# Weight folding moved to a third PSUM bank and one slot later, one ring for all weight buffers, and a later turn of the second half's rows

## The chip, the cores and the metric

The kernel runs on one core of a Trainium2 chip. The metric is the time of one execution on the device, in microseconds (us).

## The reference, cut to what matters

Three layers follow each other. The first is a gated linear attention (4 batches, 8 heads, 768 steps, head size 48): a state per head decays by a gate and takes up one outer product in each step.

```python
state = f[t] * state + k[t] (outer) v[t];  y[t] = q[t] @ state      # f = sigmoid(f_logit)
x = y as 3072 rows of 384
h = x @ w_in                      # 384 x 2048
x2 = (h * sigmoid(h)) @ w_out     # 2048 x 384
e = argmax(x2 @ w_gate)           # one of 8 experts for each row
out = prob(e) * (max(x2 @ w1[e], 0) @ w2[e])   # 384 x 1024 x 384
```

The matrices `w_in` and `w_out` of the second layer come as 64-bit floats, the others as 32-bit floats.

## The kernel before, in words

Every product of the second and the third layer is made of three products of parts: each operand is split in a rounded high part (ACT copies it) and a low part (the difference, on DVE, for some weights on POOL). So a weight buffer is always a pair, hi and lo.

**Second layer.** The 24 chunks of 128 rows form 9 groups (2, 2, six times 3, 2 chunks). A slot is one step of the second layer: nine matmuls of the first product for one slice of 128 hidden columns (`moe_h`, into one of two banks "h"), then the second product of the slice of two slots before (`moe_o`, into the banks `px` of kind "x", one for each chunk). There are 144 slots. The order is group 0 with slices 0 to 7, group 1 with slices 0 to 15, group 0 with slices 8 to 15, then the other groups. PSUM's eight banks are two "h", three "x" and three "a"; the groups 0 and 1 hold two of the three "x". What else has to be done is entered in a plan by slot: `at(slot, ...)` puts it behind the nine matmuls of `moe_h`, `at_end(slot, ...)` behind `moe_o`. The matmuls of PE run in the order in which the program writes them (`ORD = 1`). The instructions of the other engines are put in order by a scheduler which simulates times, except those that are wrapped in `keep`.

**Attention.** Six stages for each chunk run in slots ahead of the chunk's group; they use the banks "a" (the first two chunks also "h").

**Weights of the second layer.** `load_piece` fetches one slice of 128 columns of `w_in` or 128 rows of `w_out`, narrows the 64-bit numbers on DVE in three instructions, and splits. Four slices make a unit, with one buffer for hi and one for lo. The first of the three narrowing instructions is kept in program order for slices below `PI` and `PO` (12); the others are placed by the scheduler. In the profile the kept one carries L201 and the free one L320.

**Folding.** So that the second product gives the gate's logits with it, each of the 16 slices of `w_out` gets eight more columns, the slice times `w_gate`: `fold_turn` transposes the slice with six matmuls into a bank, ACT copies it (L264) into `wturn`, `fold_gate` multiplies it by `w_gate` with six matmul instructions into the same bank, then ACT writes the high part (L273) and DVE the low part (L274) of the result into the weight buffer. Slice i is folded in slot i + 3 (i below 8) or i + 11. The groups from 2 on use these columns; the logits of the groups 0 and 1 are made otherwise.

**Third layer.** The rows are scattered (POOL, `route`) into slots by expert. The largest expert known early (item 0) is begun before the second layer is at an end: its first 256 slots are the "head", its other 256 the "rest". The head's eight `up` steps and two `down` steps are written between the last steps of the second layer by the string `TAIL`: o is `moe_o`, f the next step of the head, F all that are left of them, p and r the routing of the last group, w the loading of the next expert's first weights, k the ranking of the other experts, g the fetch of the rest's rows from the slots (`xe_r`), t the turn of these rows: six transposes on PE into banks (`pxs_r`), copied by ACT and DVE to `x_r`. Then `moe2` does the rest's `up` (`p_r`) and `down` and the other experts.

**Buffers.** Weight pairs come from two rings of eight buffers each, "wa" for `in` and `w1`, "wb" for `out` and `w2` (and one buffer for `x_r`). A new unit takes the buffers that come next in its ring, once their last reader is done. The rows of the second layer's result (`x2`) rotate through five buffers.

Of the kernel before, what the change touches and what calls it, by code (L numbers as in the profile page):

```python
# [9 lines left out]
F32 = mybir.dt.float32  # L10
F32R = mybir.dt.float32r
# [10 lines left out]
P = 128  # L22
CAP = 512
ROW = 388
# [5 lines left out]
FA = 1  # L30
FB = 3
# [1 line left out]
ORD = 1  # L33
AMP = ()
STP = (1, 2, 3, 4, 5, 6, 7)
PI = 12
PO = 12
LF = -27
LV = -16
KACT = 7  # L40
ND = 1
MO = 'oeh'
TAIL = 'ofofpffrffwgffktfF'
KW = -14
HF0 = 137
FX = 0
# [45 lines left out]
def kernel(  # L92
# [16 lines left out]
    NT, DM = out.shape  # L109
    DFF = moe_w_in.shape[1]  # L110
    E, _, F2 = moe2_w1.shape
    KC = DM // P
# [12 lines left out]
    HF = NF // 2  # L125
# [5 lines left out]
    dram = ctx.enter_context(tc.tile_pool(name="dram", bufs=1, space=DRAM))  # L131
    main = ExitStack()
    ps = main.enter_context(tc.tile_pool(name="ps", bufs=1, space=PSUM))
    wts = main.enter_context(tc.tile_pool(name="wts", bufs=8))
    raw = main.enter_context(tc.tile_pool(name="raw", bufs=4))
    phase = ExitStack()
    att = phase.enter_context(tc.tile_pool(name="att", bufs=1))
    late = phase.enter_context(tc.tile_pool(name="late", bufs=1))

    def bank(kind, name):  # L140
        return ps.tile([P, 512], F32, tag=kind, name=name, bufs={"h": 2, "x": 3, "a": 3}[kind])
# [19 lines left out]
    wgc = const.tile([P, KC, E], F32, name="wgc")  # L161
# [5 lines left out]
    wturn = [side[:, ROW + i * DM : ROW + (i + 1) * DM] for i in range(2)]  # L167
# [30 lines left out]
    units = {}  # L198

    def keep(fn):  # L200
        return lambda *a, **k: tc.keep_in_program_order(fn(*a, **k))  # L201

    def new_unit(key):
        kind = key[0]
        full = [P, 4, KC, P] if kind in ("in", "w1") else [P, 4, DM + E if kind == "out" else DM]
        nm = "_".join(str(x) for x in key)
        tag = "wa" if kind in ("in", "w1") else "wb"
        units[key] = tuple(wts.tile(full, F32R, tag=tag, name=f"{nm}_{x}") for x in ("hi", "lo"))

    def part_of(src, kind, i, n):  # L210
        cols = slice(i * P, (i + n) * P)
# [15 lines left out]
    def load_piece(kind, i):  # L227
        u, h = divmod(i, 4)
        src = moe_w_in if kind == "in" else moe_w_out
        nm = f"{kind}_{i}"  # L230
        if h == 0:
            new_unit((kind, u))
        shape = [P, KC, P] if kind == "in" else [P, 1, DM]
        if src.dtype == I64:
            t = raw.tile(shape + [2], U32, tag="raw", name=f"{nm}_raw")
            made = len(pieces_made)
            pieces_made.append(i)
            load_raw(t.rearrange("p c f w -> p c (f w)"), src, kind, i, nc.scalar if made < RAW else nc.sync)
            x = raw.tile([P, ROW], U32, tag="cv", name=f"{nm}_cv", bufs=2)[:, :DM].rearrange("p (c f) -> p c f", c=shape[1])
            t2 = t.rearrange("p c f w -> p (c f) w")  # L240
            pin = keep if i < (PI if kind == "in" else PO) else lambda fn: fn
            narrow(t2, x.rearrange("p c f -> p (c f)"), pin)
            x = x.bitcast(F32)
        else:
            x = raw.tile(shape, F32, tag="raw", name=f"{nm}_raw")
            nc.sync.dma_start(out=x, in_=part_of(src, kind, i, 1))
        split((kind, u), h, x if kind == "in" else x[:, 0], nc.vector)
# [6 lines left out]
    folding = {}  # L254

    def fold_turn(i):
        u, h = divmod(i, 4)
        pt = bank("a", f"pe_{i}")
        for c in range(KC):
            for j, part in enumerate(units["out", u]):  # L260
                pe.matmul(
                    pt[:, c * P : (c + 1) * P], part[:, h, c * P : (c + 1) * P], identr, start=j == 0, stop=j == 1
                )
        nc.scalar.copy(wturn[i % 2], pt[:, :DM])  # L264
        folding[i] = pt

    def fold_gate(i):
        u, h = divmod(i, 4)
        hi, lo = (a[:, h, DM : DM + E] for a in units["out", u])
        o = folding.pop(i)[:, DM : DM + E]  # L270
        for c in range(KC):
            pe.matmul(o, wturn[i % 2][:, c * P : (c + 1) * P], wgc[:, c, :], start=c == 0, stop=c == KC - 1)
        nc.scalar.copy(hi, o)  # L273
        nc.vector.tensor_sub(lo, o, hi.bitcast(F32))  # L274

# [42 lines left out]
    def narrow(r, x, pin=lambda fn: fn):  # L318
        top, low = r[:, :, 1], r[:, :, 0]
        pin(nc.vector.tensor_scalar)(  # L320
            out=x, in0=top, scalar1=3, scalar2=0x3FFFFFF8, op0=ALU.logical_shift_left, op1=ALU.bitwise_and
        )
        nc.vector.scalar_tensor_tensor(
            out=x, in0=top, scalar=0xC0000000, in1=x, op0=ALU.bitwise_and, op1=ALU.bitwise_or
        )
        nc.vector.scalar_tensor_tensor(
            out=x, in0=low, scalar=29, in1=x, op0=ALU.logical_shift_right, op1=ALU.bitwise_or
        )
# [204 lines left out]
    def moe_o(g, i):  # L533
        hi, lo = gt.pop((g, i))
        first, last = ((0, HF), (HF - 1, NF - 1)) if g == 0 else ((0,), (NF - 1,))
        wh, wl = units["out", i // 4]
        if i in first:
            px[g] = [bank("x", f"px_{g}_{t}") for t in range(sizes[g])]
        for t in range(sizes[g]):
            w = DM if g < 2 else DM + E  # L540
            o = px[g][t][:, :w]
            m = slice(t * P, (t + 1) * P)
            pe.matmul(o, hi[:, m], wl[:, i % 4, :w], start=i in first, stop=False)
            pe.matmul(o, lo[:, m], wh[:, i % 4, :w], start=False, stop=False)
            pe.matmul(o, hi[:, m], wh[:, i % 4, :w], start=False, stop=i in last)
        if i in last:
            moe_x2(g, i)

    x2 = {}
    lgt = {}  # L550

    def moe_x2(g, i):
        lgt[g] = att.tile([P, sizes[g], E], F32, tag="lg", name=f"lg_{g}", bufs=2)
        for t in range(sizes[g]):
            n = starts[g] + t
            if n in x2:
                nc.vector.scalar_tensor_tensor(
                    out=x2[n][:, :DM], in0=px[g][t][:, :DM], scalar=0.5, in1=x2[n][:, :DM], op0=ALU.mult, op1=ALU.add
                )
                r = x2[n]  # L560
            else:
                r = att.tile([P, ROW], F32, tag="x2", name=f"x2_{n}", bufs=5)
                x2[n] = r
                if g < NG - 1 and t != 1:
                    nc.scalar.activation(r[:, :DM], px[g][t][:, :DM], AF.Copy, scale=0.5)
                else:
                    nc.vector.tensor_scalar(out=r[:, :DM], in0=px[g][t][:, :DM], scalar1=0.5, scalar2=None, op0=ALU.mult)
            if g >= 2:
                nc.vector.tensor_scalar(
                    out=lgt[g][:, t, :], in0=px[g][t][:, DM : DM + E], scalar1=0.5, scalar2=None, op0=ALU.mult  # L570
                )
            if dbg is not None and "x2" in dbg and i == NF - 1:
                nc.sync.dma_start(out=dbg["x2"][n * P : (n + 1) * P, :], in_=r[:, :DM])
        del px[g]
# [230 lines left out]
    def slots_of(k, t, n):  # L805
        return xs.rearrange("(n p) d -> n p d", p=P)[bass.ds(expert[k] * (CAP // P) + t, n)]
# [18 lines left out]
    def rest_fetch():  # L825
        nt = CAP // P - HEAD
        w = nt * P
        r = [raw.tile([P, ROW], F32, tag="cv", name=f"xe_r_{t}", bufs=2) for t in range(nt)]
        for t in range(nt):
            keep(nc.sync.dma_start)(out=r[t], in_=slots_of(0, HEAD + t, 1).rearrange("n p d -> p (n d)"))  # L830
        x = wts.tile([P, 2, KC, w], F32R, tag="wb", name="x_r")
        items["rest"] = dict(nm="r", e=0, w=w, rows=lambda t: r[t], x=[x[:, i] for i in range(2)])

    def moe2(m2):
# [267 lines left out]
    def at(slot, fn, *args):  # L1102
        plan.setdefault(slot, []).append((fn, args))

    def at_end(slot, fn, *args):
        after.setdefault(slot, []).append((fn, args))

    for n in range(NCH):
        g, r = group_of[n]
# [22 lines left out]
    for j in range(2 * NF):  # L1132
        s = VS + j * VD // 2
# [12 lines left out]
            at(s0 + RD + 3, lambda: load_ids(ranks[0], (0, 1)))  # L1146
    assert s0 + RD < len(seq)
    for i in range(NF):
        at(i + (3 if i < HF else 11), fold_turn, i)
        at_end(i + (3 if i < HF else 11), fold_gate, i)  # L1150
    def head_turn():
        head_start()
        turn(items["head"])
# [57 lines left out]
    def fill(n):  # L1211
        for fn, i in ops[:n]:
            fn(items["head"], i)
        del ops[:n]

    def preload():
# [4 lines left out]
        o=lambda: moe_o(*outs.pop(0)), f=lambda: fill(1), F=lambda: fill(len(ops)),  # L1221
        p=lambda: pick(g), r=lambda: route(g), w=preload, k=rank_rest,
        g=rest_fetch, t=lambda: turn(items["rest"]),
    )
    for c in TAIL:
        todo[c]()
# [47 lines left out]
```

## Time and profile before

| | |
|---|---|
| runs (3) | 872.99 us median, 872.1 to 876.35 |
| profiled execution | 878.09 us |
| its span | 876.4 us |
| mean granted clock of TensorE | 0.962 |
| PE busy | 839.1 us (96%) |
| DVE, ACT, POOL busy | 492.3, 383.6, 109.9 us |

The profiled execution took 1.7 us more than its span, and 5.1 us (0.6%) more than the median of the runs. A granted clock of 1.0 is 2.4 GHz, one of 0.5 is 1.2 GHz.

### The profile page before, as it was taken

What the parts mean: (1) busy time and instruction counts of PE and PEld (TensorE: products, weight loads), DVE (VectorE), ACT (ScalarE), POOL (GpSimd) and SP (SyncE); (2) the same over time, 40 slices, a digit from 0 to 9 for tenths busy, and PEclk for the clock granted to TensorE, in tenths of its full rate; (3) what the DMA queues carried; (4) which work ended last, traced back from release to release, by engine and by line L of the source; (5) the groups of instructions that cost most, each with busy time, mean ns of one, the idle gap of its engine ahead of it and who ended that gap; (6) DMA issues with size and microseconds to landing.
All of it is one profiled execution on the core that took longest, in us unless ns stands there. A gap on an engine that the chain in (4) does not pass through costs nothing. (4 is left out here: it accounts for less than half of the span.)

```text
span 876.4 us, 15480 instructions
## 1 busy us (share of the span) xinstructions
PE 839.1 (96%) x5696; PEld 801.3 (91%) x5696; DVE 492.3 (56%) x1307; ACT 383.6 (44%) x815; POOL 109.9 (13%) x144
## 2 busy tenths in 40 slices
PE   6889989999999999999999999999799999999994
PEld 3789989998999999999999999998798999999994
DVE  6886578365666565665565665366456146246520
ACT  5554455345345345345445333355245245345520
POOL 2000000000111001002001001048100110111011
PEclk9667979999999999999999999999899999999997
DMA  9763336412235325326324332314173425425400
GB/s 198 170 157 108 74 111 222 142 37 53 73 85 127 95 69 131 85 59 132 80 62 118 91 72 82 100 37 155 36 235 122 138 91 192 140 96 190 162 24 27
DMA packets 166437, 95.95 MB, mean 109 GB/s; under 512 B 115692, under 2 KB 159965, under 8 KB 166352
## 3 DMA queue, kind: packets, MB, share of 16 engines
q1 hardware_dynamic: 162224, 83.80, 36.3%
q0 software_dynamic: 3280, 9.49, 3.0%
q10 hardware_dynamic: 848, 1.57, 0.6%
q8 instruction: 47, 0.77, 0.4%
q14 instruction: 38, 0.31, 0.1%
HBM read 75.61 MB, written 16.33 MB: 105 GB/s over the span
## 5 line engine op out<-in xcount | busy, mean ns | idle before, releaser
L355 PE MATMUL px<-out_lo,gh 128*128 128x392 f32 (+1 forms) x384 | 137.8, 359 | 0.0
L519 ACT ACTIVATE se<-ph 128x384 f32<-128x384 f32 (+1 forms) x144 | 65.3, 454 | 160.6 <-PE ph L355 151.1
L355 PE MATMUL px<-out_hi,gl 128*128 128x392 f32 (+1 forms) x384 | 132.1, 344 | 1.6 <-DVE gl L530 1.6
L355 PE MATMUL px<-out_hi,gh 128*128 128x392 f32 (+1 forms) x384 | 131.7, 343 | 0.0
L521 DVE SCALAR_TENSOR_TENSOR sg<-se,ph 128x384 f32<-128x384 f32 (+1 forms) x144 | 72.8, 506 | 98.2 <-ACT se L519 98.1
L355 PE MATMUL ph<-xtl,in_hi 128*128 128x384 f32 (+1 forms) x384 | 125.0, 325 | 0.0
L355 PE MATMUL ph<-xth,in_hi 128*128 128x384 f32 (+1 forms) x384 | 124.0, 323 | 0.0
L355 PE MATMUL ph<-xth,in_lo 128*128 128x384 f32 (+1 forms) x384 | 123.8, 323 | 0.0
L530 DVE TENSOR_TENSOR gl<-sg,gh 128x384 fp32r<-128x384 f32 (+1 forms) x144 | 79.8, 555 | 36.9 <-ACT gh L529 35.8
L529 ACT CAST gh<-sg 128x384 fp32r<-128x384 f32 (+1 forms) x144 | 68.6, 477 | 64.7 <-DVE sg L521 60.7
L355 PEld LDWEIGHTS px<-out_lo,gh 128*128 128x128 f32 x384 | 73.1, 190 | 2.4 <-ACT gh L529 0.2
L355 PEld LDWEIGHTS px<-out_hi,gl 128*128 128x128 f32 x384 | 73.1, 190 | 2.3 <-DVE gl L530 2.3
L355 PEld LDWEIGHTS px<-out_hi,gh 128*128 128x128 f32 x384 | 72.9, 190 | 0.0
L355 PEld LDWEIGHTS ph<-xtl,in_hi 128*128 128x128 f32 x384 | 72.6, 189 | 0.2
L355 PEld LDWEIGHTS ph<-xth,in_hi 128*128 128x128 f32 x384 | 72.6, 189 | 0.0
L355 PEld LDWEIGHTS ph<-xth,in_lo 128*128 128x128 f32 x384 | 72.6, 189 | 0.0
L355 PE MATMUL po<-w_lo,hh 128*128 128x384 f32 (+6 forms) x200 | 68.0, 340 | 0.0
L251 ACT CAST w_hi<-w_raw 128x384 fp32r<-128x384 f32 x124 | 57.2, 514 | 23.5 <-DMA w_raw<-in_moe_w_dram 22.5
L355 PE MATMUL po<-w_hi,hh 128*128 128x384 f32 (+6 forms) x200 | 67.3, 336 | 0.0
L355 PE MATMUL po<-w_hi,hl 128*128 128x384 f32 (+6 forms) x200 | 67.3, 336 | 0.0
L252 DVE TENSOR_TENSOR w_lo<-w_raw,w_hi 128x384 fp32r<-128x384 f32 x104 | 52.8, 550 | 11.7 <-ACT w_hi L251 11.5
L355 PE MATMUL p<-xsl,w_hi 128*128 128x480 f32 (+6 forms) x168 | 58.6, 349 | 0.0
(256 smaller groups left out, 1586.6 us busy)
## 6 DMA issues: line engine op xcount, KB each, us to landing
w_raw<-in_moe_w_dram SPq DMA_DIRECT2D x64, 384.0 KB, 4.4
xs<-side SPq DMA_DIRECT2D x8, 776.0 KB, 4.6
out_again<-in_moe_w_out_dram SPq DMA_DIRECT2D x16, 384.0 KB
xe<-xs SPq DMA_DIRECT2D x7, 776.0 KB, 6.1
out_raw<-in_moe_w_out_dram SPq DMA_DIRECT2D x13, 384.0 KB
f<-in_f_logit_dram SPq DMA_DIRECT2D x24, 192.0 KB, 3.7
k<-in_k_dram SPq DMA_DIRECT2D x24, 192.0 KB, 3.4
q<-in_q_dram SPq DMA_DIRECT2D x24, 192.0 KB, 3.0
```

The lines of the kernel that those rows point to most:

```text
L251: (keep(nc.scalar.copy) if key == ("w1", 1, 1) and RT > 1 else nc.scalar.copy)(hi, x)
L252: lo_engine.tensor_sub(lo, x, hi.bitcast(F32))
L355: ins = nc.tensor.matmul(*a, **k)
L519: nc.scalar.activation(e, ph[:, :GT], AF.Tanh, scale=0.5)
L521: nc.vector.scalar_tensor_tensor(out=t, in0=e, scalar=1.0, in1=ph[:, :GT], op0=ALU.add, op1=ALU.mult)
L529: (nc.scalar.copy if g < GACT else nc.vector.tensor_copy)(hi, t)
L530: (nc.gpsimd if (g, i) < LOV else nc.vector).tensor_sub(lo, t, hi.bitcast(F32))
```

## The change

Folding takes its bank from kind "x" instead of "a", and each slice is folded one slot later (`FA` = 4, `FB` = 12). Its last two instructions, of ACT and DVE, are now a function of their own, `fold_put`, which is still called right behind `fold_gate`. The first narrowing instruction is kept in program order for all 16 slices of both matrices. The two rings of weight buffers become one of 16, so that a unit takes the buffers of the oldest unit of either kind. The rows `x2` rotate through four buffers. In `TAIL` the turn of the rest's rows (t) moves behind one more step of the head (f), which is the first of its two `down` steps.

```diff
-PI = 12
-PO = 12
+PI = 16
+PO = 16
+FA = 4
+FB = 12
...
-TAIL = 'ofofpffrffwgffktfF'
+TAIL = 'ofofpffrffwgffkftF'
...
-    wts = main.enter_context(tc.tile_pool(name="wts", bufs=8))
+    wts = main.enter_context(tc.tile_pool(name="wts", bufs=16))
...
-        tag = "wa" if kind in ("in", "w1") else "wb"
-        units[key] = tuple(wts.tile(full, F32R, tag=tag, name=f"{nm}_{x}") for x in ("hi", "lo"))
+        units[key] = tuple(wts.tile(full, F32R, tag="wt", name=f"{nm}_{x}") for x in ("hi", "lo"))
...
-        pt = bank("a", f"pe_{i}")
+        pt = bank("x", f"pe_{i}")
...
     def fold_gate(i):
         u, h = divmod(i, 4)
+        o = folding[i][:, DM : DM + E]
+        for c in range(KC):
+            pe.matmul(o, wturn[i % 2][:, c * P : (c + 1) * P], wgc[:, c, :], start=c == 0, stop=c == KC - 1)
+
+    def fold_put(i):
+        u, h = divmod(i, 4)
         hi, lo = (a[:, h, DM : DM + E] for a in units["out", u])
         o = folding.pop(i)[:, DM : DM + E]
-        for c in range(KC):
-            pe.matmul(o, wturn[i % 2][:, c * P : (c + 1) * P], wgc[:, c, :], start=c == 0, stop=c == KC - 1)
         nc.scalar.copy(hi, o)
         nc.vector.tensor_sub(lo, o, hi.bitcast(F32))
...
-                r = att.tile([P, ROW], F32, tag="x2", name=f"x2_{n}", bufs=5)
+                r = att.tile([P, ROW], F32, tag="x2", name=f"x2_{n}", bufs=4)
...
-        x = wts.tile([P, 2, KC, w], F32R, tag="wb", name="x_r")
+        x = wts.tile([P, 2, KC, w], F32R, tag="wt", name="x_r")
...
-        at(i + (3 if i < HF else 11), fold_turn, i)
-        at_end(i + (3 if i < HF else 11), fold_gate, i)
+        s = i + (FA if i < HF else FB)
+        at(s, fold_turn, i)
+        at_end(s, fold_gate, i)
+        at_end(s, fold_put, i)
```

## Rows read from the trace of the kernel before

**Rows 1.** The page: busy time by engine; granted clock in 40 slices (tenths).

```profile
PE 839.1 (96%) x5696; PEld 801.3 (91%) x5696; DVE 492.3 (56%) x1307; ACT 383.6 (44%) x815; POOL 109.9 (13%) x144
...
PEclk9667979999999999999999999999899999999997
```

**Rows 2.** Waits of PE, whole span: us in total, times, longest us.

```profile
PE py L355 <- DVE am L422: 5.9, 7, 2.5
PE pxs_r L360 <- DMA xe_r<-xs: 4.9, 1, 4.9
...
PE px L355 <- DVE gl L530: 1.6, 2, 1.2
...
PE pe L355 <- DVE xtl L500: 0.5, 1, 0.5
```

**Rows 3.** Windows: length, busy us of PE, PEld, DVE, ACT, POOL; clock; DMA.

```profile
58.30:75.15 16.85, 16.85 (x80) 16.00 (x79) 10.79 (x26) 6.56 (x18) 0.00 (x0) 0.50 0.47 120
...
117.80:129.70 11.90, 9.39 (x42) 9.14 (x41) 9.35 (x22) 3.03 (x9) 0.24 (x1) 0.58 0.34 86
...
625.70:631.60 5.90, 5.86 (x20) 5.57 (x21) 1.27 (x3) 1.12 (x3) 0.00 (x0) 0.50 0.00 1
```

**Rows 4.** Timeline of PE, end of second product, first expert: start us, length us.

```profile
620.55 0.28 PE L355 MATMUL p_h<-xeh_h,w_hi 128*128 128x256 f32 x1
625.68 1.84 PE L360 MATMUL pxs_r<-identr,xe_r 128*128 128x128 f32 x6 [4.86 <-DMA xe_r<-xs]
627.18 0.67 PE L355 MATMUL po_h<-w_lo,hh_big 128*128 128x384 f32 x1
...
633.47 0.34 PE L355 MATMUL po_h<-w_lo,hh_big 128*128 128x384 f32 x1
...
638.05 0.39 PE L355 MATMUL p_r<-x_r,w_hi 128*128 128x256 f32 x1
```

**Rows 5.** Timeline of POOL: the last group's scatters into the slots.

```profile
619.33 0.99 POOL L674 DMA_INDIRECT xs<-x,r_idx  x1 [5.50 <-DVE r_idx L667]
620.62 0.97 POOL L674 DMA_INDIRECT xs<-x,r_idx  x1 [0.30 <-issue]
```

**Rows 6.** Timeline of DVE: head's last hidden part; low parts of the rest's rows.

```profile
621.28 0.42 DVE L764 SCALAR_TENSOR_TENSOR in_q_h<-p_h,hh_side 128x256 fp32r<-128x256 f32 x1
...
627.11 1.28 DVE L750 TENSOR_TENSOR x_r<-pxs_r,x_r 128x256 fp32r<-128x256 f32 x3 [4.81 <-ACT x_r L749]
```

**Rows 7.** Windows, folding's instructions alone: one turn and gate at either clock.

```profile
64.25:65.42 1.17, 1.17 (x6) 1.17 (x6) 0.00 (x0) 0.00 (x0) 0.50 1.02 255
67.45:68.58 1.13, 1.13 (x6) 1.13 (x6) 0.00 (x0) 0.00 (x0) 0.50 0.00 0
97.53:98.25 0.72, 0.72 (x6) 0.72 (x6) 0.00 (x0) 0.00 (x0) 1.00 0.00 0
99.34:99.92 0.58, 0.58 (x6) 0.58 (x6) 0.00 (x0) 0.00 (x0) 1.00 0.65 131
```

**Rows 8.** Timeline of PE: one folding gate and the next fold's turn.

```profile
137.28 0.79 PE L355 MATMUL pe<-wgc,side 128*128 128x8 f32 x6
...
139.03 0.22 PE L355 MATMUL pe<-identr,out_hi 128*128 128x128 f32 x1
```

**Rows 9.** Timeline of DVE: narrowing of late pieces, and a fold's low part.

```profile
133.17 0.35 DVE L320 TENSOR_SCALAR out_cv<-out_raw 128x384 uint32<-128x384 uint32 x1
...
134.57 0.35 DVE L320 TENSOR_SCALAR in_cv<-in_raw 128x384 uint32<-128x384 uint32 x1
...
138.66 0.15 DVE L274 TENSOR_TENSOR out_lo<-pe,out_hi 128x8 fp32r<-128x8 f32 x1
```

**Rows 10.** Timeline of ACT: first conversion of the first expert's weights.

```profile
579.21 0.93 ACT L251 CAST w_hi<-w_raw 128x384 fp32r<-128x384 f32 x2 [0.68 <-PE ph L355]
```

**Rows 11.** Timeline of PE: end of the first output unit's last use; expert's start.

```profile
584.47 0.28 PE L355 MATMUL ph<-xtl,in_hi 128*128 128x256 f32 x1
...
610.17 0.38 PE L355 MATMUL p_h<-xel_h,w_hi 128*128 128x256 f32 x1 [0.52 <-DVE xel_h L750]
```

## The prediction

> **What bounds the kernel now.** I read the page first, then the waits of PE, then tables of windows over the stretches where PE waits or its clock is low, and at last the timelines of those stretches. The page says that PE is busy for 96% of the span, and no other engine for more than 56% [rows 1]. So the time is PE's own work, plus the time in which PE has nothing to do, plus what the granted clock costs. The row of the clock shows where that cost lies: in the first seven slices of 21.9 us and around slice 29 [rows 1]. Of the waits [rows 2] the longest single one, 4.9 us, is the turn of the rest's rows for their fetch. The waits for `am` and for `gl` belong to steps that the change leaves where they are; the 0.5 us of a folding turn for an attention bank belong to the change. Two clock stretches touch it too: 58.3 to 75.15 us at half clock, with folding in it, and 625.7 to 631.6 us, right behind the long wait [rows 3].
>
> **The turn of the rest's rows.** The last matmul of the head's last `up` starts at 620.55, and the turn's row counts 4.86 us of idle ahead of 625.68, so the idle begins at 620.82. Then PE stands still until 625.68, when the rows are there, turns them until 627.18, runs the first `down` until 633.47 and the second, with the small matmul of the flags behind it, until the rest's first `up` at 638.05 [rows 4]. That is 17.2 us. The six transposes took 1.50 us and the first `down` 6.29, since most of it ran at 0.5 [rows 3, 4]; the second `down` ran at full clock, and it and the flags took 638.05 - 633.47 = 4.58 us. The other `down`, 24 matmuls of the same shapes, then costs about 4.2 us at full clock, and the transposes about 0.75 (half of 1.50).
>
> With the change the first `down` starts at 620.8. Its last input is made at 621.28 + 0.42 = 621.70 [rows 6] and is needed only in its last three matmuls, so it isn't held up. It ends at 625.0. The rows land when they did: the two scatters start on POOL at 619.33 and 620.62, released by the index that DVE made [rows 5], and the fetch on SP's queue follows the second; none of them waits for PE's later steps. PE waits from 625.0 to 625.68, 0.7 us. In this trace waits of 1.2 us (for `gl`) and less passed inside stretches at full clock [rows 1, 2], so I take the clock to stay up. Turn to 626.4, second `down` and flags to 631.0: the rest's first `up` starts 638.05 - 631.0 = 7.1 us earlier. The copies of ACT and DVE behind the turn now have the 4.2 us of one `down` to hide in instead of two; in the trace the last low part was made at 627.11 + 1.28 = 628.39 [rows 6], 2.7 us behind the start of the turn. Everything behind (the write of the head's rows, the next fetches) hangs on the end of the second `down` and moves with it. Bounds: 7.8 us if the rows come 0.7 earlier; 4.1 us if the clock falls all the same (the half of a 5.9 us stretch given back).
>
> **Folding.** No instruction goes or comes. A turn costs 1.17 us at half clock and 0.72 at full, the six gate matmuls 1.13 and 0.58 [rows 7]. Slot 3 loses a fold and slot 11 gets one; slot 3 lies around the start of the low stretch, slot 11 at full clock. So about one fold changes from low to full clock: 2.30 - 1.30 = 1.0 us gained. The second eight folds move within full clock: nothing. The wait for an attention bank, 0.5 us [rows 2], goes. What comes is a wait that the trace of before doesn't show. With two "x" banks held by `px`, every fold uses the same third bank, so a turn must wait for the ACT and DVE instructions of the fold before. Where DVE is fullest the low part ended at 138.66 + 0.15 = 138.81 and the next turn began at 139.03 [rows 8, 9]: 0.2 us of room. Two such DVE instructions more in front (0.35 each) would make a wait of 0.5 us. I take 0.5 us in all, between nothing and 16 times 0.5 = 8 us, since the turn also has the nine matmuls of its own slot in front, as before. Sum of folding: 1.0 + 0.5 - 0.5 = 1.0 us gained. The `px` banks of the next group open only behind the nine matmuls of a slot, and their two copies fit in there: nothing. A bank of kind "a" that is free earlier may let attention start earlier; I take nothing.
>
> **Pieces in program order.** In the trace the free narrowing instructions stand nearly in that order already: only one piece of `w_out` runs before the last of `w_in`, by 1.4 us [rows 9]. Nothing, with 1.4 us either way as bounds. Behind a pinned instruction DVE's queue of `sg` and `gl` would stand, and PE behind them.
>
> **One ring.** The first expert's first unit takes the buffers of the oldest `out` unit, not of the oldest `in` unit. It was converted from 579.21 on [rows 10]; the last reader of that `out` unit ends at 584.47 [rows 11], so this starts 5.3 us later. PE needs the unit at 610.17 [rows 11], and POOL, which makes the low parts, is free for 5.50 us ahead of the scatters [rows 5]. So it's hidden; without that cover the scatters and then the turn come later, at worst by 5 us, of which the moved `down` doesn't hide any more. The units behind it take buffers freed earlier or as early, but for the first `w2` unit, two slots later, which POOL converts later still. Rows `x2` in four buffers: three are taken at a group's end, when those of the group before have been scattered for some nine slots. Nothing.
>
> **Sum.** 7.1 + 1.0 = 8.1 us: 878.1 to 870.0 for the profiled execution. It lay 5.1 us above the median of the runs, and the terms don't depend on that, so I take them from the median: 873.0 - 8.1 = 864.9.
>
> **Rivals.** (a) Faster still: the clock comes back earlier in the stretch from 58.3 to 75.15. In it the gate's tiny matmuls stand between dense blocks; with the first fold out of slot 3 the dense block there gets longer. If the clock rises 10 us earlier, half of that is gained: 860. For it: at 625.7 dense work ended the low clock after 5.9 us [rows 3], in the fold stretch it took 16.85. Against: DVE is full there, and PE may wait instead.
> (b) The tail's gain comes, and the early part gives it back: the scheduler orders ACT and DVE anew, and a wait like the one at 117.8 appears. That window of 11.9 us had a mean clock of 0.58 and PE busy 9.39 us [rows 3]; at full clock its work takes about 5 us: the price is 7. Result 872, no change.
> (c) The rows of the rest land later, because the conversions on POOL slide 5.3 us and reach into the scatters: they take 4 us of the gain, result 869. Against it are the 5.50 us [rows 5].
> (d) Slower: the single bank decides. If DVE is behind in most folds, 16 waits of 0.5 us are 8 us, and PE's small idles in that part let the clock fall once or twice, at 5 us each (11.9 times 0.42, [rows 3]): 873 - 8.1 + 8 + 10 = 883. It decides from about 0.8 us for each of 16 folds on, which is 12.8 us, the sum plus 0.5%. For it: the room is 0.2 us at one place [rows 8, 9]; against: elsewhere DVE is idle for much of the stretch, 10.79 of 16.85 us busy [rows 3].
>
> The Trainium skill (TensorE: Matmul & The Clock Gate, section "A second HAM failure mode: psum-queue depth-cycling") speaks against this change. It tells of a kernel that cycled through PSUM banks, where short idles between groups of matmuls were enough to swing the clock. By that rule (d) is what happens, at 883 instead of 864.9. No row of before shows such a swing: folding ran there with the clock at 1.0 [rows 7] as well as at 0.5.
>
> **How the numbers follow.** Forecast 0.45, (a) 0.2, (b) 0.17, (c) 0.08, (d) 0.1. The predicted time is the forecast's, 865. The range reaches from (a), less 2 us for the spread of the runs, to (b): 858 to 872. It leaves out (d) and the tails of (a). Forecast, (a) and half of (c) and a little of (b) are faster by more than 0.5% (under 868.6; less can't be told from no change): 0.71. Slower is (d), less some of it: 0.08. The rest, 0.21, is no change.
>
> **What would show it.** Right: the first `down` of the head follows its last `up` without idle, the turn's wait is below 1 us, and the clock stays at 1.0 until the rest's first `up`, 10 to 11 us behind the head's last `up`. Folding's turns wait for L274 for under 1 us in all. Conversions of the first expert's weights start near 584 and PE's expert start doesn't wait for them. Wrong: a turn wait of 3 us or more, a low clock behind it, waits of folding turns for L274, or a new low stretch ahead of 170 us.

## The result, and the profile after

| | before | after |
|---|---|---|
| runs | 872.99 us median | 865.6 us median (864.64 to 866.23) |
| ratio, with its 95% interval | | 0.9908 [0.9882, 0.9933] |
| profiled execution | 878.09 us | 865.60 us |
| its span | 876.4 us | 863.9 us |
| mean granted clock | 0.962 | 0.975 |
| PE busy | 839.1 us | 826.0 us |

The changed kernel is 0.9% faster, 7.4 us between the medians. One of its five executions took 2391.78 us; the range and the ratio leave it out, nothing on record says what slowed it, and none of the seven executions run later was like it. The two profiled executions lie 12.5 us apart. In the page of the changed kernel (busy time by engine, clock in 40 slices) more of the early slices are high than in [rows 1], and the dip at slice 29 is gone:

```profile
PE 826.0 (96%) x5696; PEld 790.2 (91%) x5696; DVE 492.2 (57%) x1307; ACT 384.0 (44%) x815; POOL 109.9 (13%) x144
...
PEclk8789979999999999999999999999999999999997
```

The third and fourth slice are at 8 and 9 where [rows 1] has 6 and 7, and the slice with the tail is at 9 instead of 8. The waits of PE (in total, times, longest) show what became of the turn's wait:

```profile
PE py L360 <- DVE am L427: 6.8, 9, 1.8
PE pl L360 <- ACT lfh L353: 3.3, 1, 3.3
PE px L360 <- DVE gl L535: 3.1, 3, 2.5
...
PE pxs_r L365 <- DMA xe_r<-xs: 0.9, 1, 0.9
PE pk L365 <- ACT qt L407: 0.7, 1, 0.7
```

The turn waited 4.9 us in [rows 2] and waits 0.9 here. This list of all waits down to 0.7 us has no line with `pe`: no folding turn waited for the fold before it, nor for an attention bank.

The timeline of PE over the tail answers to [rows 4]:

```profile
615.33 0.28 PE L360 MATMUL p_h<-xeh_h,w_hi 128*128 128x256 f32 x1
615.44 0.34 PE L360 MATMUL po_h<-w_lo,hh_big 128*128 128x384 f32 x1
...
620.73 1.15 PE L365 MATMUL pxs_r<-identr,xe_r 128*128 128x128 f32 x6 [0.95 <-DMA xe_r<-xs]
621.64 0.42 PE L360 MATMUL po_h<-w_lo,hh_big 128*128 128x384 f32 x1
...
626.31 0.39 PE L360 MATMUL p_r<-x_r,w_hi 128*128 128x256 f32 x1
```

The first `down` starts right behind the head's last `up`, and the turn follows it. A window over the same stretch (length, busy time of PE and the others, clock) has PE busy for 9.97 of 11 us, all of it at full clock, where [rows 3] has 5.9 us at 0.5:

```profile
615.40:626.40 11.00, 9.97 (x59) 9.02 (x58) 2.52 (x13) 2.13 (x6) 1.96 (x2) 1.00 0.28 92
```

Three differences make up the 12.5 us. The head's last `up` starts at 615.33 against 620.55 [rows 4], so 5.2 us were already there ahead of the tail. From that matmul to the rest's first `up` it is 10.98 us against 638.05 - 620.55 = 17.50: 6.5 us. From there to the span's end it is 237.6 us against 238.35: 0.8 us. The 7.4 us between the medians leave no room for the first term as a gain of the change. That was the first thing to settle.

### The profile page after: what moved, and what is told of

Same layout as the page of the kernel before. It is cut to its first block, busy times and chain, and to the rows that moved or that the text cites. A ratio compares the mean times of both kernels' runs of the same rounds, so it can differ in the third digit from the quotient of the medians.

```text
span 863.9 us, 15479 instructions
## 1 busy us (share of the span) xinstructions
PE 826.0 (96%) x5696; PEld 790.2 (91%) x5696; DVE 492.2 (57%) x1307; ACT 384.0 (44%) x815; POOL 109.9 (13%) x144
## 4 chain that ended last, share of the span: by engine, by line
PE 66%; issue 10%; DMA 10%; DVE 5%; ACT 4%; SPq 2%; POOL 1%; POOLq 0%; DVEq 0%; ACTq 0%
PE px L360 20%; PE ph L360 19%; DMA out_dram<-o,oi 6%; PE p L360 5%; PE py L360 5%; PE po L360 4%; PE pe L360 2%; PE sc L360 2%; POOL w_lo L253 1%; PE pl L360 1%; PE pq L365 1%; PE p_r L360 1%; PE pk L365 1%; PE po_r L360 1%; DMA f<-in_f_logit_dram 1%
```

## The experiments

**The tail alone, and all but the tail.** Two kernels, the one from the kernel before and the other from the changed one:

```diff
--- before, the tail alone
-TAIL = 'ofofpffrffwgffktfF'
+TAIL = 'ofofpffrffwgffkftF'
--- changed kernel, the tail undone
-TAIL = 'ofofpffrffwgffkftF'
+TAIL = 'ofofpffrffwgffktfF'
```

> The kernel before with the turn of the rest's rows one step of the head later, and nothing else of the change. Theory T (the turn is the gain): the changed kernel's own trace puts the stretch from the head's last up to the rest's first up at 10.9 us instead of 17.2, so 6.3 us are gained here: 866.7 us for 873.0, ratio 0.991 to 0.994. Theory E (the early part, with folding, gives a good part of the 7.4 us between the medians): the turn alone gives at most 4 us, ratio 0.9955 or above.

> The changed kernel with the old order of the turn; folding, pieces in order, ring and row buffers stay changed. Theory T: within 1.5 us of the kernel before, ratio 0.998 to 1.002, with a wait of the turn of 4 to 5 us and a low clock behind it. Theory E: 3 us or more below before, ratio 0.9965 or less, since the early part's gain is kept.

The tail alone: 865.82 us, 0.9919 [0.9889, 0.9948], which is 7.1 us of 872.47. All but the tail: 872.89 us, 0.9996 [0.9976, 1.0016]. So the moved turn is the gain that the times show; by its interval, all the rest together lies between 2.1 us gained and 1.4 lost. The timeline of PE with the tail alone shows the same pattern as the changed kernel's, 10.89 us from the last `up` to the rest's first. With the tail undone that is 17.7 us, with a wait of 4.96 us and 6.1 us at a clock of 0.50 behind it.

```profile
621.41 0.28 PE L355 MATMUL p_h<-xeh_h,w_hi 128*128 128x256 f32 x1
621.53 0.34 PE L355 MATMUL po_h<-w_lo,hh_big 128*128 128x384 f32 x1
...
626.53 0.30 PE L360 MATMUL pxs_r<-identr,xe_r 128*128 128x128 f32 x1 [0.63 <-DMA xe_r<-xs]
627.11 0.77 PE L360 MATMUL pxs_r<-identr,xe_r 128*128 128x128 f32 x5 [0.27 <-DMA xe_r<-xs]
...
632.30 0.39 PE L355 MATMUL p_r<-x_r,w_hi 128*128 128x256 f32 x1
```

This profiled execution took 871.68 us although its tail is short: it comes to the tail at 621.41, as late as before's does in [rows 4].

**The folding alone, and the kernel before once more.** The kernel before with the third "x" bank and the later slots; and the kernel before itself, unchanged:

```diff
-        pt = bank("a", f"pe_{i}")
+        pt = bank("x", f"pe_{i}")
...
-        at(i + (3 if i < HF else 11), fold_turn, i)
-        at_end(i + (3 if i < HF else 11), fold_gate, i)
+        at(i + (4 if i < HF else 12), fold_turn, i)
+        at_end(i + (4 if i < HF else 12), fold_gate, i)
```

> The kernel before with folding in the bank of kind x and one slot later, nothing else. Theory T: my sum's 1.0 us or nothing, ratio 0.997 to 1.001. Theory E: 3 us or more below before, ratio 0.9965 or less. Rival D (the single bank makes turns wait and the clock swing): slower, ratio over 1.005.

> The kernel before, unchanged, profiled a second time. Theory R (the profiled execution of before had an unlucky early clock): the executions of one program differ by up to 5 us in their spans, higher mean clock going with the shorter span, and this profile reaches the last folding turn up to 5 us earlier than 163.75 us. Against R: it reaches that turn within 1 us of 163.75, and the 5 us between the two early parts belong to the change. Ratio 0.998 to 1.002 in either case.

The folding alone: 873.37 us, 1.0006 [0.9987, 1.0025]. Before again: 872.21 us, 0.9992 [0.9976, 1.0008]. The folding is worth nothing that the medians show, and the same program came to the tail 4.8 us earlier in this profiled execution than in the one of [rows 4], at 615.75 against 620.55 (to the last folding turn 6.7 us earlier, at 157.07 against 163.75, which is more than the 5 us that I had allowed). The window says where. It is the kernel before again, over the stretch that has a clock of 0.50 in [rows 3]:

```profile
58.30:75.15 16.85, 16.29 (x146) 15.37 (x146) 15.39 (x39) 10.11 (x27) 0.00 (x0) 1.00 0.71 174
```

Here the clock was 1.00. So the low stretch of 16.85 us belongs to some executions of the program and not to all, and the 5.2 us ahead of the tail are no part of the 7.4 us between the medians.

**One ring alone, and all pieces in program order alone**, each from the kernel before:

```diff
--- one ring
-    wts = main.enter_context(tc.tile_pool(name="wts", bufs=8))
+    wts = main.enter_context(tc.tile_pool(name="wts", bufs=16))
...
-        tag = "wa" if kind in ("in", "w1") else "wb"
+        tag = "wt"
...
--- in program order
-PI = 12
-PO = 12
+PI = 16
+PO = 16
```

The first also has four buffers for the rows `x2`, and takes `x_r` from the one ring.

> The kernel before with one ring of 16 weight buffers and four row buffers, nothing else. Theory T and my sum: nothing, ratio 0.998 to 1.002; the first expert's weights are converted some 5 us later than 579 us in a span like that of before, and its first product doesn't wait for them. Against it: the conversions on POOL slide into the scatters and the wait of the turn grows by up to 4 us, ratio 1.003 or more. Theory B (an upper band of some 878 us, in which the clock stays low around 58 to 75 us, belongs to the old folding): one or two of some twelve executions lie there.

> The kernel before with all weight pieces in program order, nothing else. My sum: nothing, ratio 0.998 to 1.002; on DVE the last piece of w_in is narrowed ahead of the piece of w_out that preceded it. Against it: a pinned piece holds up DVE's queue and PE behind it, ratio 1.003 or more. Theory B: one or two of some twelve executions lie near 878 us.

One ring: 872.38 us, 0.9997 [0.9968, 1.0026]. In program order: 872.60 us, 0.9994 [0.9967, 1.0021]. Neither changes the time beyond its interval, which reaches up to 2.9 us either way. What I expected on DVE came: the last piece of `w_in` is narrowed from 131.89 on, the piece of `w_out` behind it from 132.23. The later conversions that I expected of the ring didn't come as I had them (more on this below).

**The two halves of the folding, one at a time.** The changed kernel with the old slots and the third "x" bank; and with the new slots and a bank of kind "a":

```diff
--- old slots
-FA = 4
-FB = 12
+FA = 3
+FB = 11
--- a bank
-        pt = bank("x", f"pe_{i}")
+        pt = bank("a", f"pe_{i}")
```

> The changed kernel with folding in its old slots, but still in the bank of kind x. Theory T: the time of the changed kernel, ratio 0.989 to 0.994. Theory B in the form that the later slot takes the upper band away: one or two of some twelve executions lie 5 to 6 us above the others. In the form that the bank does it: none.

> The changed kernel with folding in its new slots, but in the banks of kind a as before. Theory T: the time of the changed kernel, ratio 0.989 to 0.994. Theory B in the form that the later slot takes the upper band away: no execution lies 5 to 6 us above the others. In the form that the bank does it: one or two of some twelve do.

With the old slots: 869.03 us, 0.9959 [0.9925, 0.9993], and 5 of its 12 executions between 870.7 and 877.7. That misses theory T's 0.989 to 0.994, though the intervals of the two kernels overlap, and there are more high executions than the one or two of theory B. With a bank of kind "a": 867.22 us, 0.9922 [0.9893, 0.9950], the highest 869.2, as expected. The wait that I had feared of the single bank came with the old slots. In this kernel's timeline of PE the second fold's turn stands at 63.61, held until DVE has written the low part of the first fold:

```profile
58.23 0.22 PE L360 MATMUL pe<-identr,out_hi 128*128 128x128 f32 x1
...
63.61 0.33 PE L360 MATMUL pe<-identr,out_hi 128*128 128x128 f32 x1 [1.32 <-DVE out_lo L279]
...
64.18 0.42 PE L360 MATMUL pe<-identr,out_hi 128*128 128x128 f32 x1
...
66.63 1.28 PE L360 MATMUL pe<-wgc,side 128*128 128x8 f32 x6
```

The timeline of DVE says why: that low part of 0.15 us ran at 63.40, behind a row of instructions of 0.35 to 0.55 us without a gap.

```profile
61.72 0.35 DVE L203 TENSOR_SCALAR out_cv<-out_raw 128x384 uint32<-128x384 uint32 x1
61.99 0.55 DVE L380 TENSOR_TENSOR kpad<-k,en 128x384 f32<-128x384 f32 x1
62.46 0.55 DVE L331 SCALAR_TENSOR_TENSOR out_cv<-out_raw,out_cv 128x384 uint32<-128x384 uint32 x1
62.93 0.55 DVE L379 TENSOR_TENSOR qpad<-q,ep 128x384 f32<-128x384 f32 x1
63.40 0.15 DVE L279 TENSOR_TENSOR out_lo<-pe,out_hi 128x8 fp32r<-128x8 f32 x1
```

The windows of this kernel, ahead of the second turn and from it on, show what followed. PE was busy for 3.82 of 5.31 us at full clock, and then ran 13.9 us at 0.51:

```profile
58.30:63.61 5.31, 3.82 (x29) 3.29 (x27) 5.31 (x15) 4.13 (x11) 0.00 (x0) 1.00 0.70 184
63.61:77.50 13.89, 13.21 (x62) 12.35 (x63) 8.41 (x20) 4.82 (x11) 0.00 (x0) 0.51 0.59 143
```

At full clock the work of that window takes about half of its 13.21 us, so by this estimate the low clock cost some 6.5 us, five times the wait ahead of it. In the kernel before again, which has the old slots too and waited as long for `qpad` (1.2 us), no turn waited that long and the clock stayed at 1.00.

**The turn at other places.** One step later still than in the changed kernel, behind both `down` steps, and one step earlier than in the kernel before, ahead of the head's last `up`:

```diff
--- changed kernel, turn last
-TAIL = 'ofofpffrffwgffkftF'
+TAIL = 'ofofpffrffwgffkfFt'
--- before, turn earlier
-TAIL = 'ofofpffrffwgffktfF'
+TAIL = 'ofofpffrffwgfktffF'
```

> The changed kernel with the turn of the rest's rows one step later still, behind both downs of the head. Theory T (what the turn waits for is only the rows; behind it stand the copies): the wait for the fetched rows, 0.95 us in the changed kernel, goes, and in its place the rest's first up waits for the copies, which there is no down to hide any more: in the kernel before the last low part was made 2.7 us behind the start of the turn, and the transposes take 0.9, so 1.3 to 1.9 us of idle. Sum: 0.3 to 1 us longer than the changed kernel, ratio to the kernel before 0.991 to 0.994. Rival L (the later the turn, the better: the copies are early enough by themselves): the 0.95 us go and nothing comes, ratio 0.989 to 0.990.

> The kernel before with the turn of the rest's rows one step earlier, ahead of the head's last up. Theory T (the time of the landing is set by POOL and SP, whatever PE does): the turn waits for the rows one up longer, about 4.9 + 1.1 = 6 us, and the up that was ahead of it runs behind it: the idle grows by 1.1 us, but the up itself is only moved, so the time is the same to 1.5 us longer, the up running at the low clock behind the wait (ratio 1.000 to 1.002). Rival Q (the landing hangs on the head's steps): the wait stays at 4.9 us and the landing comes 1.1 us earlier, ratio 0.998 to 1.000.

Turn last: 865.74 us, 0.9918 [0.9894, 0.9943]. Its timeline has the wait for the rows gone, and 0.70 us for the copies in its place:

```profile
614.49 0.28 PE L360 MATMUL p_h<-xeh_h,w_hi 128*128 128x256 f32 x1
...
622.94 0.82 PE L365 MATMUL pxs_r<-identr,xe_r 128*128 128x128 f32 x6
623.69 0.38 PE L360 MATMUL pf<-identr,bad 128*1 128x128 f32 x2
624.77 0.39 PE L360 MATMUL p_r<-x_r,w_hi 128*128 128x256 f32 x1 [0.70 <-DVE x_r L755]
```

The stretch is 10.28 us, 0.7 shorter than in the changed kernel, where theory T had it 0.3 to 1 us longer: I had expected 1.3 to 1.9 us of exposed copies. In the trace, then, T's sign was wrong. The time can't tell: the ratio lies in the range of T, and the two kernels' intervals overlap. Turn earlier: 874.84 us, 1.0021 [0.9994, 1.0048], with the wait at 5.92 us, as theory T had it. The turn began 5.07 us behind the start of the second scatter (613.49 to 618.56) and in [rows 4, 5] 5.06 us, so moving the turn ahead doesn't bring the rows sooner.

**The later slots alone, and the changed kernel once more**, for the spread of executions:

```diff
--- before, later slots in the old banks
-        at(i + (3 if i < HF else 11), fold_turn, i)
-        at_end(i + (3 if i < HF else 11), fold_gate, i)
+        at(i + (4 if i < HF else 12), fold_turn, i)
+        at_end(i + (4 if i < HF else 12), fold_gate, i)
```

> The kernel before with the folds one slot later, and still in the attention's banks. Theory B in its slot form (the executions that take 5 to 6 us more belong to the old slots, whatever the bank): none or one of 20 executions lies above 876, where the kernel before has some 1 in 6; the median is 0 to 1 us below, ratio 0.998 to 1.000. In its bank form, or if the upper band is chance: as many executions above 876 as in the kernel before beside it, ratio 1.000.

> The changed kernel once more, for its spread. Theory B: all 20 executions lie within 864 to 869, none 5 us above; ratio 0.990 to 0.992. If the upper band is chance and has nothing to do with the folding: 2 to 4 of 20 lie at 870 to 872, and the median is the same.

Later slots alone: 873.93 us, 1.0004 [0.9985, 1.0022], 12 executions between 871.58 and 875.67. The changed kernel again: 867.63 us, 0.9932 [0.9907, 0.9957], 7 executions between 865.61 and 868.58. Its ratio lies above the expected 0.990 to 0.992, and its gain is 5.9 us here. The kernel before beside them had 873.79 us, 3 of 29 above 877. With 12 and 7 executions in place of 20, and none of 12 high in the kernel before again, no single kernel settles theory B; taken together they speak for its slot form. Executions more than 3 us above the median of their set: 24 of 166 with the old slots, 1 of 68 with the new ones, in whichever bank. The expectations spoke of 5 to 6 us; more than 5 us above it are 16 and none. The old slots' count includes the 4 of the kernel with the single bank. The mean hardly moves all the same: 873.7 us with the later slots alone, 873.8 in the kernel before beside it.

The clock in the profiled executions shows what such an execution meets. In all 14 of them PE waits for attention's `qpad` near 55, and in 7 the clock is low within some 3 us behind that wait. How long it stays down differs. Windows over the low stretches, in this order: tail alone (old slots), in program order alone (old slots), the changed kernel, the folding alone:

```profile
57.50:75.15 17.65, 17.61 (x84) 16.77 (x84) 11.22 (x28) 7.22 (x18) 0.00 (x0) 0.52 0.52 122
```

```profile
55.00:59.00 4.00, 3.82 (x18) 3.77 (x19) 4.00 (x11) 3.33 (x9) 0.00 (x0) 0.57 0.82 149
```

```profile
55.50:59.00 3.50, 3.50 (x16) 3.50 (x15) 3.50 (x10) 3.50 (x9) 0.00 (x0) 0.54 0.88 165
```

```profile
57.50:61.00 3.50, 3.50 (x16) 3.50 (x15) 3.50 (x9) 2.36 (x6) 0.00 (x0) 0.55 0.96 234
```

The long ones, here, in [rows 3] and in the kernel with the old slots above, have folding gates in them (x6 matmuls of 1.28 us at half clock, at 60.71 and 67.11 with the tail alone). The short ones end before the first gate, which stands at 59.79 in the second kernel, at 61.73 in the changed one and at 62.90 in the last. The difference, some 13 us at half clock, is by the same estimate 6.5 us of time, about what the executions that stand out take more. The third long one, with the single bank, began behind the 1.32 us of the turn. That the gates hold the clock down is argued from this order in time; that the long stretches occur with the old slots (in 3 of 7 profiled executions) and didn't in the 7 with the new ones is shown.

## Why the prediction was right, step by step

**The turn: right, and it is the gain.** Predicted 7.1 us. Done alone it measured 7.1 by the ratio (0.81%, interval 0.52% to 1.11%) and 6.65 between the medians; by the traces the stretch got 6.5 us shorter. So the equal 7.1 is in part luck. The missing half microsecond is the sum of small ones. The rows landed 5.40 us behind the last `up`'s start where I had carried over 5.13 from [rows 4], so the wait is 0.95 and not 0.68. The transposes took 0.91 us and not half of 1.50. The second `down` with the flags took 4.67 against 4.58, the first 4.34 against 4.2; the start without idle gave 0.16 back. The step on which most hung, that the clock stays up over the wait that is left, held: 1.00 in the window with 0.95 us, and still with 1.21 us in the changed kernel's second profile.

**The folding: 1.0 us predicted, nothing measured.** Alone it gave 1.0006 [0.9987, 1.0025], that is 0.5 us lost, between 1.1 gained and 2.2 lost. The step that failed is "about one fold changes from low to full clock": I read the low stretch of one execution as the program's. In the kernel before run again the same folds ran at full clock. The removed 0.5 us of an attention bank is real in the trace, and the 0.5 us set against it for L274 didn't come; with the measured spread neither can be told in the time.

**The pieces and the ring: nothing in the time, as predicted, but one reason was wrong.** I had the first expert's conversion start 5.3 us later, near 584, in the buffers of the oldest `out` unit. It starts at 574.59, which is 40.7 us ahead of the head's last `up`, against 41.3 before [rows 4, 10]. The timelines of ACT and POOL in the changed kernel, and between them two lines of PE:

```profile
574.59 0.93 ACT L252 CAST w_hi<-w_raw 128x384 fp32r<-128x384 f32 x2 [0.69 <-PE ph L360]
575.70 0.92 ACT L252 CAST w_hi<-w_raw 128x384 fp32r<-128x384 f32 x2
...
579.71 1.75 ACT L252 CAST w_hi<-w_raw 128x384 fp32r<-128x384 f32 x4 [0.28 <-PE px L360]
```

```profile
574.39 0.28 PE L360 MATMUL ph<-xth,in_hi 128*128 128x256 f32 x1
...
579.69 0.34 PE L360 MATMUL px<-out_hi,gh 128*128 128x392 f32 x1
```

```profile
595.75 12.72 POOL L253 TENSOR_TENSOR w_lo<-w_raw,w_hi 128x384 fp32r<-128x384 f32 x12 [3.52 <-PE px L360]
614.22 0.99 POOL L679 DMA_INDIRECT xs<-x,r_idx  x1 [5.75 <-DVE r_idx L672]
```

The two lines of PE are the last matmuls of slice 3 of the last group, in the first and in the second product: the last readers of the oldest `in` unit and of the oldest `out` unit. The first four conversions were released by the first product, as in [rows 10], and ended before slice 3 of the second product began (578.79). So the first unit still takes the oldest `in` unit's buffers, and not, as I had it, those of the oldest `out` unit; these go to the next unit, whose four conversions follow together when the last reader is done. With the ring alone the first conversion starts 40.75 us ahead of the head's last `up`, much as in the changed kernel. POOL's 5.75 us of room ahead of the scatters is as large as in [rows 5].

**The base: right.** The sum was taken from the median, 873.0, and not from the profiled 878.1. Taken from the latter it would have given 870.0, 4.4 us too much; before again showed that most of that distance was an unlucky clock of the execution. That 864.9 came within 0.7 us of 865.6 is luck in part: the 1.0 us of the folding didn't come, and the changed kernel run again had a median of 867.63.

**The rivals.** (a) may have its mechanism but not its price: with the later slots the gates stand behind the low stretch, and most executions of 3 us and more above the median are gone, which neither the median nor the mean shows as a gain. (b) came as a wait without its price: some 20 us ahead of the tail `px` waits 2.5 us for `gl` in each of the seven profiled kernels with one ring, and at most 1.3 in the seven with two. One line of PE from the ring alone, and one from the kernel before:

```profile
591.46 0.44 PE L355 MATMUL px<-out_hi,gl 128*128 128x392 f32 x1 [2.50 <-DVE gl L530]
```

```profile
598.21 0.45 PE L355 MATMUL px<-out_hi,gl 128*128 128x392 f32 x1 [1.25 <-DVE gl L530]
```

The clock stayed at 1.00 around it, with the ring alone (586 to 594 us) and in the changed kernel (588 to 596), and the ring alone cost nothing that the time shows (0.9997). (c) didn't come: POOL kept its room. (d) didn't come either, since the changed kernel has no fold that waits.

The section of the Trainium skill that the prediction names (TensorE: Matmul & The Clock Gate, section "A second HAM failure mode: psum-queue depth-cycling") tells of idles between groups of matmuls, frequent enough that the clock went up and down. The folding alone shows nothing of the kind: no turn waited, and it took 873.37 us and not 883. With the same single bank and the old slots, though, one wait of 1.32 us was followed by 13.9 us at half clock: a single fall behind a single idle, the nearest to it that a run here shows.

It seems to be the later slots that make the single bank harmless: in the changed kernel's timelines the first fold's gate ran from 61.73 to 62.46, its low part from 62.69 to 62.86, and the next turn started at 66.43, so DVE had 3.6 us of room. Later folds had less, the least 0.56 us (155.46 to 156.02).

## What to carry to other kernels

Where PE stands idle for data that come at a fixed time, put work that is ready in front of the wait; the gain is the idle plus the low clock behind it, here 3.9 (4.86 - 0.95) and about 2.6 us of the 6.5. Before costing a low clock, see whether it is there in another execution of the same program, and subtract from the median of the runs. A median can hide a change that removes only the highest of the times: look at the spread and the mean too.

## What the runs showed that was not expected

The same program ran its stretch from 58.3 to 75.15 us once at a clock of 0.50 and once at 1.00, and came to its tail 4.8 us apart. What decides it is open. Where the clock fell within some 3 us behind attention's wait for `qpad`, in seven profiled executions, that wait was 2.0 to 2.7 us; in six of the other seven it was 1.0 to 1.2. But its length doesn't decide it alone: in the kernel with the turn last, the waits of PE show 2.5 us of it,

```profile
PE pq L365 <- DVE qpad L379: 2.5, 1, 2.5
```

and the clock stayed at 0.98 on the mean from 50 to 75 us, while the changed kernel fell to half speed for 3.5 us behind 2.6 us of the same wait. It wasn't tried to take that wait away.
